# Zero matmuls between the last V product and the first scores, and token pairs on one partition: a fused attention and MLP block on one core

## The chip, the cores and the metric

The kernel runs on one core of a Trainium2 chip. The metric is device time in microseconds (us) of a whole execution. A profiled execution has a span, from its first instruction to its last, and a time of its own that lies a little above it.

The engines are named as the profile names them: PE is TensorE's matmuls and PEld its weight loads, DVE is VectorE, ACT is ScalarE, POOL is GpSimd, and SPq is SyncE's queue, which issues every DMA here.

## The reference

Input x has 2048 tokens of 512 features, in bf16. It is normalised, and attention with one shared K and V head and a GELU MLP are both applied to the same normalised x; both results are added to x.

```python
xn = _layernorm(x)                                    # 2048 x 512
# A: 32 query heads of 16, one K head and one V head
q = (xn @ wq).reshape(B, S, 32, 16)
k, v = xn @ wk, xn @ wv                               # 2048 x 16 each
p = softmax(einsum("bhqd,bkd->bhqk", q, k) * 16 ** -0.5)
a = einsum("bhqk,bkd->bhqd", p, v).reshape(B, S, 512) @ wo
# B: 512 -> 1792 -> 512
m = gelu(xn @ w1 + b1) @ w2 + b2
out = x + a + m
```

## The kernel before

**Stages.** A prologue loads x (16 tiles of 128 tokens), normalises it, transposes it (xnT), and makes K, V and the first group's Q. The main loop follows: 4 blocks of 512 queries, 8 groups of 4 heads in each, 16 key tiles. A tile of work is 128 keys by 512 queries of one head, and three tiles make a unit `u`, of which there are 683. For each unit TensorE computes scores into three banks of PSUM (`scores`, line 1009: three matmuls on different rows of the array), the exponential of two thirds of them is done on ScalarE (`exp`, line 1032) and of the rest on VectorE and GpSimd by integer arithmetic (`Dt`, lines 1063, 1106, 1110), and TensorE multiplies with V into one accumulator bank (`pv_mm`, line 1076). Banks 0 to 2 take the even units' scores and banks 3 to 5 the odd ones'. The Q, MLP and output products of each block (line 682) are spread among the units at due times; two GELU passes on ScalarE stand at units 182 and 512.

**What sets the order.** A recorder, `Prog`, collects every instruction with what it reads and writes. `Prog.schedule` then plays the program against a table of durations and due times and fixes one order for each engine. `Prog.emit` writes that order out, with one semaphore for each engine and for each DMA stream, so that at run time each engine works through its own list and waits where the list says so. The scheduler knows one kind of work that no data needs: `filler` and `pro_filler`, matmuls with a tile of zeros. In the prologue it inserts `pro_filler` (512 columns into bank 3) until the last V product has been placed (`s_seen`), in the main loop `filler`. Between the last V product and the first scores it inserts nothing.

**The prologue in its order.** SyncE issues nine loads of x, two with one tile and seven with two tiles, then wk, wv, wq, w1 (rows of 1792 elements), b1, w2, wo. A tile's statistics are taken on VectorE (line 782, then `mv`, line 796) or ScalarE (line 779); the reciprocal root is made on ScalarE (`lnv` and `rstd`, lines 800 and 802); the normalised tile is written by VectorE (line 815) or ScalarE (line 814), transposed by TensorE (line 827) and copied to `xnT` (line 831). V products are `v_tiles` (line 896, recorded at line 676). At the end the largest |k|, needed for the exponent's bias, is found: VectorE reduces to `kmx` (line 944), TensorE transposes it (line 945), VectorE reduces to `kmr` (line 947), TensorE spreads it over the partitions with `crow` (line 948, recorded at line 676), VectorE makes the bias `krow` (line 949), and only then is K copied to `KT` with the bias added (lines 849 and 850), on which the first scores wait. ScalarE writes V to its table meanwhile (line 962), and GpSimd writes five scaled copies of it (line 967).

**Tokens and partitions.** Token `t * 128 + p` lies on partition `p` of tile `t`, so a load of two tiles reads two runs of 1 KB for each partition:

```python
x_view = xf.rearrange("(t p) d -> p t d", p=P)
o, src, w = x_sb[:, a:b, :], x_view[:, a:b, :], [("x", ti) for ti in range(a, b)]
```

In the main loop x is loaded again, tile by tile (`x_load`), to be added to the output, and each output tile is stored as it is done (`store`).

Of the kernel before, what the change touches and what calls it, by code (L numbers as in the profile page):

```python
# [10 lines left out]
P = 128  # L11
# [42 lines left out]
LAL = 30.0  # L54
LCO = 0.0
PRO_FROM = 2.0
TBL = 1
DMASK = {".": (), "0": (0,), "2": (2,), "a": (0, 1), "b": (1, 2), "x": (0, 1, 2),
         "o": (0,), "t": (2,), "A": (0, 1), "B": (1, 2), "X": (0, 1, 2)}
# [55 lines left out]
class Prog:  # L115
# [116 lines left out]
    def schedule(self):  # L232
# [16 lines left out]
        order = []  # L249
# [22 lines left out]
        def seen(o):  # L272
            return max(o.rdy + (PL_TAKE if o.kind == "pl" else 0.0), lockend) if o.lock else o.rdy

        while left:
            best_e, best_t = None, None
            for e in engs:
# [5 lines left out]
                t = max(free[e], min([seen(o) for o in able[e]] if not pro else [0.0]))  # L283
# [3 lines left out]
            e, t = best_e, best_t  # L287
            cand = [o for o in able[e] if seen(o) <= t + 1e-9]
            if e == "pe":
                op = self.pick_pe(t, cand, ready["pe"], mode, visit, cgbusy)  # L290
                st = max([free["pe"]] + cgbusy) if mode == "col" else max([free["pe"], pend + SWITCH] + cgbusy)
# [3 lines left out]
                lim = min([o.rdy for o in ready["pe"] if o.kind == "S"] + [t + 9.0]) if op is None else t  # L295
                if op is None and self.pro_filler and not s_seen and st < PRO_FROM:
                    free["pe"] = st + 0.05
                    continue
                if op is None and self.pro_filler and not s_seen and low:
                    f = _Op()  # L300
                    f.eng, f.stream, f.amt, f.need, f.ticket, f.kind = "pe", "pe", 1, False, None, "fill"
                    f.deps, f.fn, f.tag = list(self.fill_deps), self.pro_filler, (None, 0)
                    pace = [o for o in order[-40:] if o.eng in ("dve", "act") and o.vis <= st]
                    if pace:
                        pace = max(pace, key=lambda o: o.vis)
# [22 lines left out]
                if FILL_GAP and tgt and low and st > FILL_FROM and lim - st > FILL_GAP:  # L328
                    for cg in range(4):
                        f = _Op()  # L330
# [15 lines left out]
                if op == "idle":  # L346
                    op = None
# [4 lines left out]
            else:  # L352
                op = min(cand, key=self.due)
# [40 lines left out]
            if e == "pe":  # L394
                vleft -= op.kind == "v"
                s_seen = s_seen or vleft == 0
                st = t
                if op.kind in ("pv", "side"):
                    cg = op.tag[1]
                    st = max(t, cgbusy[cg], free["pe"])  # L400
                    if mode != "col":
                        st = max([t, pend + SWITCH] + [c + SWITCH for c in cgbusy])
# [17 lines left out]
                elif op.kind != "side":  # L420
                    m = {"S": "row", "side": "col"}.get(op.kind, "full")
                    w = SWITCH if m != mode else 0.0
                    st = max([t, pend + w] + [c + w for c in cgbusy])
# [30 lines left out]
            for o, cross in op.outs:  # L454
                o.nun -= 1
                v = op.vis if cross else op.end
                if v > o.rdy:
                    o.rdy = v
                if o.nun == 0:
                    ready[o.eng].append(o)  # L460
        last = {}
        for op in order:
            if op.kind == "pv":
# [6 lines left out]
        self.ncold = ncold  # L470
        self.span = max(o.vis for o in order)
        self.ops = order

    def settle(self):
        free = {e: 0.0 for e, _ in self.SECTIONS}
        mode, cg, pend, aend = None, [0.0] * 4, 0.0, 0.0
        for op in self.ops:
            occ = op.occ
            lat = 0.0 if op.kind == "fill" else op.lat
            t = max([free[op.eng]] + [o.real for o in op.deps])  # L480
            if op.eng == "pe":
                if op.kind in ("pv", "side") or (op.kind == "fill" and occ > 0.15):
                    t = max(t, cg[op.tag[1]]) if mode == "col" else max([t, pend + SWITCH] + [c + SWITCH for c in cg])
                    cg[op.tag[1]] = t + 0.216
                    mode, end = "col", t + 0.006
                else:
                    m = "row" if op.kind == "S" else "full"
                    w = SWITCH if m != mode else 0.0
                    t = max([t, pend + w] + [c + w for c in cg])
                    mode, end = m, t + occ  # L490
                pend = t + occ
            else:
                end = t + occ
            free[op.eng] = max(free[op.eng], end)
            op.real = t + occ + lat
            if op.kind in ("exp", "gelu"):
                aend = max(end + A_LAG, aend + occ + A_INC)
                op.real = aend + A_SEM
# [47 lines left out]
def bass_parallel_sum__grouped_kv_mqa__dense_activation_gelu__prompt_kernel(  # L546
# [13 lines left out]
    xf = A_x.flatten_outer_dims()  # L560
    of = out.flatten_outer_dims()
    S, D = xf.shape
# [17 lines left out]
    with ExitStack() as es:  # L580
        def sb(shape, dtype, name):
            return es.enter_context(nc.sbuf_tensor(name, shape, dtype))

        x_sb = sb([P, NT, D], bf, "x_sb")
# [19 lines left out]
        zeros = sb([P, P], bf, "zeros")  # L604
# [46 lines left out]
        def bank(b, n=1):  # L651
            return pAll[:, b * 512:(b + n) * 512]

        pO, pM = bank(6), bank(7)
        pr = Prog(nc)
# [3 lines left out]
        def B(b):  # L659
            return ("bank", b)  # L660
# [27 lines left out]
        def dma(eng, o, i, stream, r=(), w=(), lat=2.2, allow=1.0, occ=0.7, **kw):  # L688
            return add(eng, lambda e: e.dma_start(o, i), r, w, dma=stream, occ=occ, lat=lat, allow=allow, **kw)
# [6 lines left out]
                return act(fa, r=ra, w=w, n=na, lat=la, due=due, tag=alt)  # L696
            return dve(fd, r=rd, w=w, n=nd, mode=mode, due=due, tag=alt)

        x_view = xf.rearrange("(t p) d -> p t d", p=P)
        nd = 0  # L700
        for a, b, t in X_D:
            nd += 1
            if a is None:
                o, src, w = ((wvk[:, :, Dh:2 * Dh], A_wk, ["wk_s"]), (wvk[:, :, 0:Dh], A_wv, ["wv_s"]))[b]
                src = src.rearrange("(k p) n -> p k n", p=P)
            else:
                o, src, w = x_sb[:, a:b, :], x_view[:, a:b, :], [("x", ti) for ti in range(a, b)]
            dma("sp", o, src, f"d_i{nd}", w=w, lat=t - 0.47 * nd, due=0.0, occ=0.47)
        dma("sp", wq_sb[:], A_wq.rearrange("(k p) n -> p k n", p=P), "d_wq", w=["wq"], due=0.4, lat=8.0)
        dma("sp", w1_sb[:], B_w1.rearrange("(k p) n -> p k n", p=P), "d_w1", w=["w1"], due=0.5, lat=9.0)  # L710
# [3 lines left out]
        def setup(fn, r=(), w=(), occ=0.16, due=0.0, lat=0.1, **kw):  # L714
# [20 lines left out]
              w=[(k, g, j) for k in ("QT", "QTm") for g in range(NGR) for j in range(HG)])  # L735
        setup(lambda e: e.tensor_copy(wkp[:, :, :, 0:Dh], wvk[:, :, Dh:2 * Dh].unsqueeze(2).to_broadcast([P, DT, 4, Dh])),
              r=["wk_s", "wkp"], w=["wkp"], occ=0.35, due=2.0)
# [8 lines left out]
              r=["mrow"], w=["isc"], due=10.0)  # L746
# [10 lines left out]
        for gl in range(2):  # L757
            setup(lambda e, gl=gl: e.tensor_copy(sel_diag[gl], mask8[:, 4 * gl:4 * gl + 4].unsqueeze(1).to_broadcast([P, NGR // 2, HG])),
                  r=["mask8", "sel8"], w=["sel8"], due=12.0)
# [96 lines left out]
        def vbank(a, b):  # L856
            return (pO[:, a * 32:b * 32], "O") if a < NVA else (bank(5)[:, (a - NVA) * 32:(b - NVA) * 32], B(5))
# [32 lines left out]
        def vsrc(a, b):  # L890
            return vbank(a, b)[0].rearrange("p (t n) -> p t n", n=32)[:, :, 0:Dh]
# [49 lines left out]
        for ft, bk in H_PRO:  # L941
# [8 lines left out]
            r=["khm", "kcm"], w=[B(3), "kb", "krow"], n=40, due=0.0)  # L950
# [5 lines left out]
        for va, vb_ in ((0, NVA), (NVA, NT)):  # L956
            src = vsrc(va, vb_)
            ad(lambda e, src=src, va=va, vb_=vb_: e.activation(Vf[:, va:vb_, :], src, ACT.Copy),
               lambda e, src=src, va=va, vb_=vb_: e.tensor_copy(Vf[:, va:vb_, :], src), (vb_ - va) * Dh, (vb_ - va) * Dh,
               w=[vbank(va, vb_)[1], ("Vf", va)], due=DU["vf"])  # L960
            r = ["V1", ("Vf", va)]
            ad(lambda e, va=va, vb_=vb_: e.activation(V1[:, 0, va:vb_, 0:Dh], Vf[:, va:vb_, :], ACT.Copy),
               lambda e, va=va, vb_=vb_: e.tensor_copy(V1[:, 0, va:vb_, 0:Dh], Vf[:, va:vb_, :]), (vb_ - va) * Dh, (vb_ - va) * Dh,
               w=[("V", 0, va)], ra=r, rd=r, mode=2, due=DU["vf"] + 0.1)
        for v in KV_ORD:
            c = SPL_C[v]
            f = lambda e, v=v, c=c: e.tensor_scalar(V1[:, 1 + v, :, 0:Dh], Vf, c, None, ALU.mult)
# [282 lines left out]

        def x_load(tb, i):
            ti = tb * 4 + i
            dma("sp", x_sb[:, 14 + i % 2, :], x_view[:, ti, :], f"d_xr{i % 2}", w=[("x", 14 + i % 2)], lat=2.5)

        def store(tb, i, src, key):
            ti = tb * 4 + i
            dma("sp", of[ti * P:(ti + 1) * P, :], src, f"d_o{i}", r=[key], w=[("ob", i)])

        def out_tile(tb, i):
            y_mm(tb, i, al=Y_ALLOW)  # L1260
            wo_mm(tb, i, range(NGR // 2), al=Y_ALLOW)
            b2_mm(al=Y_ALLOW)
            xr, key = x_sb[:, 14 + i % 2, :], ("x", 14 + i % 2)
            dve(lambda e: e.tensor_tensor(xr, pM, xr, ALU.add), w=[key] + M4, allow=EV_ALLOW)
            store(tb, i, xr, key)
# [100 lines left out]
        for i in range(4):  # L1366
            mm4(bank(FB[i]), oT[:, i * P:(i + 1) * P], wol[:, :], False, True,
               r=[("oTl", i // 2), "wol"], w=[B(FB[i])], due=0.0)
        for i in (0, 1, 3, 2):
            dst, key = ub[:, 6 + i, :], ("u", 0, 6 + i)  # L1370
            w = [(B(FB[i]), j) for j in range(4)] + ([B(FB[i])] if i < 3 else []) + [key]
            if i < 3:
                dve(lambda e, i=i, dst=dst: e.tensor_tensor(dst, bank(FB[i]), xpy[:, i, :], ALU.add),
                    r=[("u", 0, 2 * i), ("u", 0, 2 * i + 1)], w=w)
            else:
                act(lambda e, i=i, dst=dst: e.activation(dst, bank(FB[i]), ACT.Copy), w=w)
            store(tb, i, dst, key)
        pr.in_chain = False
        if PRO_FROM:
            zr = bass.AP(zeros[:].tensor, zeros[:].offset, [list(zeros[:].ap[0]), [0, 4], [1, P]])  # L1380
            pr.pro_filler = lambda e: e.matmul(bank(3), zeros[:], zr, start=True, stop=True, skip_group_check=True)
        if FILL_GAP:
            pr.filler = lambda e, j, o: e.matmul((pO if o else pM)[32 * j:32 * j + 32, :], zeros[:, 0:32], xnT[:, 0, 0:TBW],  # L1383
                                                 start=not o, stop=not o, skip_group_check=True,
# [37 lines left out]
```

## Time and profile before

| | us |
|---|---|
| median of 3 runs | 748.96 |
| lowest and highest | 748.05, 751.28 |
| profiled execution, its own time | 749.08 |
| its span | 747.4 |
| PE, DVE, ACT, POOL busy | 732.1, 731.5, 730.2, 384.6 |
| mean granted TensorE clock | 0.993 of full speed |

In the profile a row of the timeline gives the start, the length, the engine, the line, what is written and read, how many instructions are merged, and in brackets how long the engine was idle before it and what released it. Line 676 stands for all ordinary matmuls of the prologue and line 682 for the products in column groups, since helpers record them; the operands tell them apart. Line 1381 is `pro_filler`. A row of windows gives for a stretch of time how long each engine was busy in it; PEclk is the share of TensorE's full clock that was granted. A busy time of matmuls includes the tail of each one.

### The profile page before, as it was taken

The numbers are of one execution on the slowest core, as the hardware profiler recorded it, in microseconds if no ns is written. First come the engines' busy times: TensorE is split into PE (matmuls) and PEld (weight loads), VectorE is DVE, ScalarE is ACT, GpSimd is POOL, SyncE is SP. The second block draws the span as 40 slices with busy tenths as digits, with TensorE's granted clock in tenths as the row PEclk, the third lists the DMA queues.
The fourth block names the chain that finished last, engine by engine and source line by source line (L and its number), as shares of the span: only waits on it lengthen the run. The fifth ranks groups of instructions, "written<-read, shape, count | busy, mean of one in ns | idle before, by whom it ended". The sixth has DMA issues, their size and how long they took to land.

```text
span 747.4 us, 22083 instructions
## 1 busy us (share of the span) xinstructions
PE 732.1 (98%) x9033; PEld 214.1 (29%) x9033; DVE 731.5 (98%) x1412; ACT 730.2 (98%) x741; POOL 384.6 (51%) x548
## 2 busy tenths in 40 slices
PE   8999999999999999999999999999998999999998
PEld 4222222222233222222222222222232222222223
DVE  7899999999999999999999999999999999999996
ACT  7799999999999999999999999999999999999995
POOL 7434555555533556555656455444544656546560
PEclk9899999999999999999999999999999999999999
DMA  9200100000020010100101010100100101010011
GB/s 302 71 15 22 28 13 17 24 9 17 16 46 22 18 38 18 23 17 14 25 14 27 25 39 16 36 18 14 24 13 24 30 18 38 16 46 18 10 31 36
DMA packets 32094, 23.34 MB, mean 31 GB/s; under 512 B 16385, under 2 KB 27514, under 8 KB 31994
## 3 DMA queue, kind: packets, MB, share of 16 engines
q1 hardware_dynamic: 31994, 21.94, 11.3%
q8 instruction: 72, 1.18, 0.7%
q14 instruction: 28, 0.23, 0.1%
HBM read 13.08 MB, written 2.35 MB: 21 GB/s over the span
## 4 chain that ended last, share of the span: by engine, by line
ACT 61%; PE 23%; DVE 15%; issue 1%; DMA 0%; SPq 0%
ACT E L1032 61%; PE pAll L1076 10%; PE pAll L1009 7%; DVE Dt L1063 6%; PE pAll L682 5%; DVE Dt L1110 5%; DVE stats L782 1%; PE pAll L676 1%; DVE ub L815 1%; DVE Of L1122 1%; DMA x_sb<-in_A_x_dram 0%; PE pAll L1383 0%; DVE Dt L1106 0%; DVE x_sb L1218 0%; DVE xnT L831 0%
## 5 line engine op out<-in xcount | busy, mean ns | idle before, releaser
L1032 ACT ACTIVATE E<-pAll 128x1024 bf16<-128x1024 f32 (+1 forms) x676 | 681.0, 1277 | 3.5 <-PE pAll L1009 3.4
L1106 POOL TENSOR_SCALAR Dt<-Dt 128x512 int16<-128x512 int16 x454 | 343.6, 757 | 327.0 <-DVE Dt L1110 117.6
L1076 PE MATMUL pAll<-Dt,V 128*32 128x512 bf16 x2775 | 409.7, 385 | 2.6 <-DVE Of L1122 2.3
L1063 DVE TENSOR_SCALAR Dt<-pAll 128x512 int16<-128x512 f32 (+1 forms) x541 | 368.9, 696 | 3.7 <-PE pAll L1009 2.6
L1076 PE MATMUL pAll<-E,V 128*32 128x512 bf16 x1493 | 304.5, 384 | 0.2 <-DVE Of L1122 0.2
L1110 DVE TENSOR_SCALAR Dt<-Dt 128x1024 int16<-128x1024 int16 (+6 forms) x540 | 289.4, 562 | 0.4
L1009 PE MATMUL pAll<-QT,KT 32*128 32x512 bf16 x2048 | 268.0, 386 | 5.2 <-ACT E L1032 2.1
L1009 PEld LDWEIGHTS pAll<-QT,KT 32*128 32x128 bf16 x2048 | 66.6, 91 | 296.5 <-ACT E L1032 282.6
L1076 PEld LDWEIGHTS pAll<-Dt,V 128*32 128x32 bf16 x2775 | 103.2, 95 | 102.7 <-issue 69.1
L1076 PEld LDWEIGHTS pAll<-E,V 128*32 128x32 bf16 x1493 | 72.7, 94 | 44.6 <-issue 33.5
L682 PE MATMUL pAll<-xnT,w_sb 128*32 128x512 bf16 x896 | 84.8, 383 | 0.0
L682 PE MATMUL pAll<-w_sb,x_sb 128*32 128x512 bf16 x448 | 76.4, 384 | 0.0
L682 PE MATMUL pAll<-w_sb,ub 128*32 128x512 bf16 x448 | 64.3, 383 | 0.1
L682 PE MATMUL pAll<-wop,oTp 128*32 128x512 bf16 x256 | 51.9, 383 | 0.0
L1153 POOL TENSOR_TENSOR oTp<-OfP,rbP 128x256 bf16<-128x256 f32 (+1 forms) x28 | 22.5, 809 | 14.6 <-DVE Dt L1110 7.9
L682 PEld LDWEIGHTS pAll<-xnT,w_sb 128*32 128x32 bf16 x896 | 21.3, 95 | 26.8 <-issue 17.0
L682 PE MATMUL pAll<-xnT,wq_sb 128*32 128x512 bf16 x256 | 26.8, 383 | 0.0
L1106 DVE TENSOR_SCALAR Dt<-Dt 128x512 int16<-128x512 int16 x101 | 26.5, 284 | 0.0
L1122 DVE COPY Of<-pAll 128x512 f32<-128x512 f32 x31 | 21.2, 682 | 0.1
L1218 DVE TENSOR_SCALAR x_sb<-pAll,b1T 128x512 bf16<-128x512 f32 x28 | 20.8, 742 | 0.0
L1218 DVE TENSOR_SCALAR ub<-pAll,b1T 128x512 bf16<-128x512 f32 x28 | 20.7, 739 | 0.0
L682 PEld LDWEIGHTS pAll<-w_sb,x_sb 128*32 128x32 bf16 x448 | 18.3, 94 | 8.2 <-issue 6.7
(123 smaller groups left out, 264.5 us busy)
## 6 DMA issues: line engine op xcount, KB each, us to landing
OfP<-Of SPq DMA_DIRECT2D x124, 32.0 KB, 2.0
rbP<-rden_rows SPq DMA_DIRECT2D x124, 32.0 KB, 1.8
w_sb<-in_B_w_dram SPq DMA_DIRECT2D x2, 1792.0 KB, 11.3
x_sb<-in_A_x_dram SPq DMA_DIRECT2D x18, 128.0 KB, 2.2
QT<-qp SPq DMA_DIRECT2D x124, 16.0 KB, 1.8
x_sb<-in_A_x_dram SPq DMA_DIRECT2D x7, 256.0 KB, 4.4
out_dram<-x_sb SPq DMA_DIRECT2D x12, 128.0 KB, 2.0
wq_sb<-in_A_wq_dram SPq DMA_DIRECT2D x1, 512.0 KB, 5.8
```

Of the source, the lines that this page charges most:

```text
L676: return add("pe", lambda e: e.matmul(o, l, rh, start=start, stop=stop, **kw), r, w, occ=occ, lat=dlat[1], allow=allow, **ak)
L682: add("pe", lambda e, c=c, j=j: e.matmul(o[c, :], l[:, c], rh, start=start, stop=stop, tile_position=(0, 32 * j)), r, [(k, j) for k in w] ...
L782: dve(lambda e, ti=ti, c=c: e.bn_stats(stats[:, c, :], x_sb[:, ti, :]), r=[("x", ti)], w=[("st", ti)], n=557, due=land(ti) + DU["sd"])
L1009: ins = e.matmul(o, l, rh, start=True, stop=True, tile_position=(q0, 0))
L1032: o = act(lambda e: e.activation(E[:, s0:s0 + na, :], bank(b0, na).rearrange("p (a n) -> p a n", a=na), ACT.Exp, scale=LN2 / 128.0), w=[B( ...
L1063: op = dve(lambda e: e.tensor_scalar(Dt[:, s:s + n, :], bank(bk, n).rearrange("p (a n) -> p a n", a=n), float(127 * 128) + SPL_D, SPL_MIN, ...
L1076: add("pe", lambda e, a, b: e.matmul(pO[32 * j:32 * j + 32, :], V1[:, v, kt, :], rhs, start=a, stop=b, tile_position=(0, 32 * j)), r=r + [ ...
L1106: add("pool", lambda e, d=d, k=k: e.tensor_scalar(d, d, 1.0, float(k), ALU.mult, ALU.add), [], [(("D", base[o > 0] + q), o)], occ=PL_OCC, ...
L1110: dve(lambda e, d=view(o, nb), q=view(i, nb), k=k: e.tensor_scalar(d, q, float(k), None, ALU.add), r=keys(i), w=keys(o), n=nb * n * TBW, m ...
L1122: dve(lambda e: e.tensor_copy(Of[:, i, :], pO), w=["O", ("Of", i)], allow=0.0)
L1153: "pool", lambda e, c=c: e.tensor_tensor(oTp[0:n, sl, c], OfP[0:n, s, c], rbP[0:n, s, c], ALU.mult),
L1218: dve(lambda e: e.tensor_scalar(ubs[tb % 2][:, ft, :], pM, b1T[:, ft:ft + 1], None, ALU.add), r=["b1T"], w=M4 + [ukey(tb, ft)], n=TBW + 57 ...
```

## The change

**Fill.** After the order is fixed, a new pass, `fill_gaps`, walks through it. From the last V product to the first scores it puts as many zero matmuls of 256 columns into each planned gap of TensorE as fit at 0.13 us each. They write to half of bank 2, which the first scores overwrite. Each waits for the newest VectorE or ScalarE instruction that should be done by then, so that it runs at its place in the gap and not ahead of it.

**Tokens.** Tokens 2p and 2p+1 of a block of 256 now lie on partition p, in two neighbouring tiles. A load of two tiles reads one run of 2 KB for each partition. A single tile, and a store, moves rows of 1 KB that lie 2 KB apart. Attention does not depend on the order of the keys, and queries go back to their own tokens in the store.

```diff
+GAP_BANK = 2
...
+        order = self.fill_gaps(order)
...
+    def fill_gaps(self, order):
+        t0 = min(o.start for o in order if o.kind == "S")
+        t1 = max(o.end for o in order if o.kind == "v")
+        ew = [o for o in order if o.eng in ("dve", "act") and o.start < t0]
+        s0 = min((o for o in order if o.kind == "S"), key=lambda o: o.start)
+        out, end = [], None
+        for op in order:
+            if op.eng == "pe" and op.start <= t0:
+                if end is not None:
+                    for i in range(int((op.start - end - 0.1) / 0.13)):
+                        st = end + 0.05 + 0.13 * i
+                        f = _Op()
...
+                        f.deps, f.fn, f.tag = list(self.fill_deps), self.gap_filler, (None, 0)
+                        f.occ = 0.107
+                        f.start, f.end, f.vis = st, st + f.occ, st + f.occ + 0.2
+                        pace = [o for o in ew if o.vis <= st]
+                        if pace:
+                            pace = max(pace, key=lambda o: o.vis)
+                            pace.need = True
+                            f.deps.append(pace)
+                        f.deps += [o for o in s0.deps if o.vis <= st and o.eng != "pe"]
...
+                        out.append(f)
+                if op.start >= t1:
+                    end = max(end or 0.0, op.start + op.occ)
+            out.append(op)
+        return out
...
-        x_view = xf.rearrange("(t p) d -> p t d", p=P)
+        x_view = xf.rearrange("(t p a) d -> p t a d", p=P, a=2)
+        o_view = of.rearrange("(t p a) d -> p t a d", p=P, a=2)
...
-                o, src, w = x_sb[:, a:b, :], x_view[:, a:b, :], [("x", ti) for ti in range(a, b)]
+                o, src, w = x_sb[:, a:b, :], (x_view[:, a // 2, :, :] if b - a == 2 else x_view[:, a // 2, a % 2:a % 2 + 1, :]), [("x", ti) for ti in range(a, b)]
...
-            dma("sp", x_sb[:, 14 + i % 2, :], x_view[:, ti, :], f"d_xr{i % 2}", w=[("x", 14 + i % 2)], lat=2.5)
+            dma("sp", x_sb[:, 14 + i % 2, :], x_view[:, ti // 2, ti % 2, :], f"d_xr{i % 2}", w=[("x", 14 + i % 2)], lat=2.5)
...
-            dma("sp", of[ti * P:(ti + 1) * P, :], src, f"d_o{i}", r=[key], w=[("ob", i)])
+            dma("sp", o_view[:, ti // 2, ti % 2, :], src, f"d_o{i}", r=[key], w=[("ob", i)])
...
+            zg = bass.AP(zeros[:].tensor, zeros[:].offset, [list(zeros[:].ap[0]), [0, 2], [1, P]])
+            pr.gap_filler = lambda e: e.matmul(bank(GAP_BANK)[:, 256:512], zeros[:], zg, start=True, stop=True, skip_group_check=True)
```

TensorE's list before, from the last eight V products to the second set of scores (`tk_dve`, `tk_act` and `tk_pool` are the semaphores of VectorE, ScalarE and GpSimd; `kmx` and `kmr,crow` are the two small matmuls of the maximum; the four between are a K product):

```order
L676 MATMUL pAll<-wvk,xnT 128x32 x7
L676 MATMUL pAll<-xnT,oTp 128x512 x4
L945 MATMUL pAll<-ident_f,kmx 1x128 [waits tk_dve]
L676 MATMUL pAll<-kmr,crow 128x1 [waits tk_dve]
L1009 MATMUL pAll<-QT,KT 128x512 [waits tk_dve]
L1009 MATMUL pAll<-QT,KT 128x512 x2
```

The same place in the changed kernel:

```order
L708 MATMUL pAll<-wvk,xnT 128x32 x7
L708 MATMUL pAll<-xnT,oTp 128x512 x4
L978 MATMUL pAll<-ident_f,kmx 1x128 [waits tk_dve]
L1415 MATMUL pAll<-zeros 128x256 [waits tk_act]
L1415 MATMUL pAll<-zeros 128x256
L1415 MATMUL pAll<-zeros 128x256 [waits tk_act]
L708 MATMUL pAll<-kmr,crow 128x1 [waits tk_dve]
L1415 MATMUL pAll<-zeros 128x256 x4
L1415 MATMUL pAll<-zeros 128x256 [waits tk_dve]
L1415 MATMUL pAll<-zeros 128x256
L1042 MATMUL pAll<-QT,KT 128x512 [waits tk_dve]
L1042 MATMUL pAll<-QT,KT 128x512 x2
```

Three fills stand ahead of the `kmr,crow` matmul and six behind it. The first waits for ScalarE's first write of V to its table (line 962 before), the third for its second write, the eighth for `krow`. Every other row of TensorE's list keeps its place, and the lists of VectorE, ScalarE and GpSimd are the same in both kernels.

On SyncE's list the loads of x change their shape, here before:

```order
L689 DMA x_sb<-in_A_x_dram 128x512 x2
L689 DMA x_sb<-in_A_x_dram 128x2x512 x7
L689 DMA wvk<-in_A_wk_dram 128x4x16
L689 DMA wvk<-in_A_wv_dram 128x4x16
L689 DMA wq_sb<-in_A_wq_dram 128x4x512
```

and in the changed kernel:

```order
L721 DMA x_sb<-in_A_x_dram 128x512 x2
L721 DMA x_sb<-in_A_x_dram 128x1024 x7
L721 DMA wvk<-in_A_wk_dram 128x4x16
L721 DMA wvk<-in_A_wv_dram 128x4x16
L721 DMA wq_sb<-in_A_wq_dram 128x4x512
```

Seven loads go from 256 runs of 512 elements to 128 runs of 1024, and nothing on SyncE's list moves.

More of the change, by code (lines that the diff above doesn't have):

```diff
@@ L472, in schedule @@
         self.ops = order
+    def fill_gaps(self, order):
[10 more added lines that the diff above has]
+                        f = _Op()
+                        f.eng, f.stream, f.amt, f.need, f.ticket, f.kind = "pe", "pe", 1, False, None, "fill"
+                        f.deps, f.fn, f.tag = list(self.fill_deps), self.gap_filler, (None, 0)
[7 more added lines that the diff above has]
+                        f.deps += [o for o in s0.deps if o.vis <= st and o.eng != "pe"]
+                        for o in f.deps:
+                            o.need = True
+                        out.append(f)
[3 more added lines that the diff above has]
+        return out
     def settle(self):
```

## The prediction

> **What bounds the kernel now.** I read the page first, then the chain that ended last in order of time, then busy time by windows of 3.4 us, then the timeline of the places that these pointed at.
>
> ```profile
> PE 732.1 (98%) x9033; PEld 214.1 (29%) x9033; DVE 731.5 (98%) x1412; ACT 730.2 (98%) x741; POOL 384.6 (51%) x548
> ACT 61%; PE 23%; DVE 15%; issue 1%; DMA 0%; SPq 0%
> ```
>
> From the page: three engines are busy 98% of the span, and the chain changes between them. The main loop has no slack to win, and the change touches nothing in it. What the change can move is the stretch ahead of it: the loop starts earlier, or its first microseconds run faster. The chain of waits in order of time shows what that stretch hangs on (start, length, what):
>
> ```profile
> 1.71 3.53 DMA x_sb<-in_A_x_dram
> ...
> 5.26 1.29 DVE stats L782 x2
> ...
> 20.04 0.61 DVE xnT L831
> ...
> 23.11 0.36 DVE KT L850
> ...
> 29.07 0.54 PE pAll L1009 x3
> ...
> 30.42 0.35 PE pAll L1009 x3
> ...
> 30.79 1.45 ACT E L1032
> ```
>
> Three pieces: the third x load (tiles 2 and 3), issued at 1.71, which lands at 5.24; VectorE from 5.26 to 20.65 without a break (every piece left out there is DVE); then TensorE, from the first scores, once KT is made at 23.11, up to the sixth exp at 30.79. In that last piece a score step costs 0.54 on the chain, and at 30.42 only 0.35. The windows say why (length; busy us of PE, PEld, DVE, ACT, POOL with counts; granted TensorE clock; DMA share; GB/s):
>
> ```profile
> core 0: us, PE busy (x) PEld busy (x) DVE busy (x) ACT busy (x) POOL busy (x), PEclk, DMA share, GB/s
> 9.60:13.00 3.40, 2.71 (x46) 1.94 (x43) 3.40 (x10) 3.21 (x9) 3.09 (x16) 1.00 1.07 377
> 19.80:23.20 3.40, 2.04 (x22) 0.94 (x22) 2.44 (x9) 1.58 (x9) 1.13 (x2) 1.00 0.77 244
> 23.30:26.60 3.30, 3.08 (x14) 0.70 (x14) 2.17 (x5) 2.50 (x4) 3.14 (x6) 0.50 0.03 10
> 26.60:30.00 3.40, 3.40 (x16) 0.55 (x14) 2.31 (x4) 2.32 (x3) 0.94 (x2) 0.50 0.05 10
> 30.10:33.50 3.40, 3.40 (x36) 0.98 (x34) 3.40 (x7) 3.29 (x4) 0.53 (x1) 1.00 0.04 10
> 565.90:569.30 3.40, 1.14 (x23) 0.60 (x25) 3.40 (x7) 3.38 (x3) 0.00 (x0) 1.00 0.04 10
> 569.40:572.70 3.30, 3.30 (x30) 1.47 (x22) 3.30 (x7) 3.07 (x3) 0.00 (x0) 0.50 0.09 21
> ```
>
> The clock was halved from 23.2 to 30.0, after a stretch of 3.4 us in which TensorE was busy for 2.04 only. Stretches with 2.71 and more kept it whole. It was halved once more at 569.4, after a stretch with 1.14. So the threshold lies between 2.04 and 2.71 by this measure.
>
> **The fill.** It adds nine matmuls of 256 columns and takes nothing away. TensorE's timeline in the gap:
>
> ```profile
> 20.91 1.02 PE L676 MATMUL pAll<-xnT,oTp 128*128 128x512 bf16 x4
> 21.94 0.27 PE L945 MATMUL pAll<-ident_f,kmx 128*1 128x128 f32 x1
> 22.58 0.17 PE L676 MATMUL pAll<-kmr,crow 1*128 1x1 bf16 x1 [0.38 <-DVE kmr L947]
> 23.52 1.03 PE L1009 MATMUL pAll<-QT,KT 32*128 32x512 bf16 x6 [0.76 <-DVE KT L850]
> ```
>
> Four matmuls of 512 columns take 1.02, and of that about 0.17 is the tail (the one of a single column takes 0.17), so 0.21 for 512 columns, and 0.107 for 256. Three fills stand in the 0.38 of idle time (0.32), six in the 0.76 (0.64). Before 23.20 the gap leaves 0.38 and 0.45 idle; with both filled, 2.04 becomes some 2.8, on the side of 2.71. Fills are zeros, and zeros count, as the program's start shows:
>
> ```profile
> 8.34 1.02 PE L1381 MATMUL pAll<-zeros 128*128 128x512 bf16 x3 [0.47 <-ACT lnv L800]
> ```
>
> At 8.34 three matmuls of 512 columns take 1.02, and two waits lie among them. At half clock they would be 3 x 0.43 and a tail, 1.46. Behind them lie only the zero matmuls and four transposes, so zeros had brought the clock up.
>
> What the halved clock costs is read from ScalarE, with GpSimd's copies of V beside it:
>
> ```profile
> 21.58 0.67 ACT L962 ACTIVATE V<-oTp 128x224 bf16<-128x224 f32 x2
> 24.17 1.94 ACT L1032 ACTIVATE E<-pAll 128x1024 bf16<-128x1024 f32 x2 [0.38 <-PE pAll L1009]
> 26.53 1.02 ACT L1032 ACTIVATE E<-pAll 128x1024 bf16<-128x1024 f32 x1 [0.42 <-PE pAll L1009]
> ...
> 29.66 2.58 ACT L1032 ACTIVATE E<-pAll 128x1024 bf16<-128x1024 f32 x2 [0.48 <-PE pAll L1009]
> ```
>
> ```profile
> 24.91 2.71 POOL L967 TENSOR_SCALAR V<-oTp 128x256 bf16<-128x256 f32 x3
> ```
>
> At full clock the first scores are done 0.2 earlier (0.54 against 0.35), so the first exp starts at 23.97. Two exps back to back take 1.94, one alone 1.02: 0.92 each. The sixth then starts at 23.97 + 5 x 0.92 = 28.57 instead of 30.79: 2.2 us. TensorE is not late: its 7.27 us from 23.52 to 30.79 shrink to 3.6, against 4.6 of exps. VectorE was idle for 3.30 - 2.17 and 3.40 - 2.31 in the two stretches at half clock, 2.2 together, so it too can come 2.2 earlier and no more. GpSimd's copies of V end 24.91 + 0.9 for the first of three, at 25.8; the V products that wait for it stand just ahead of the score step of 29.07 and come some 1.5 earlier, to about 26.5, so they are covered by 0.7. I take 2.1. The bounds are 0 (the clock falls anyway) and 2.2.
>
> What the fills may cost: the third waits for ScalarE's second V write, which ends at 22.25, and the crow matmul behind it (22.58) starts the chain krow, KT, first scores. With the fill itself, 0.107, that is 22.36, and 0.2 of cover is left, less what the semaphore takes. The eighth waits for krow; at 23.11 KT is made from krow, in 0.36, and the first scores wait for that, so the last two fills (0.21) fit in ahead of them. So nothing at full clock, and up to 0.5 at half clock, where six fills take 1.28 and not 0.64.
>
> A rule against it: the Trainium skill, "TensorE: Matmul & The Clock Gate", section "Why this matters for your kernels", asks for no idle gaps over about 3 us between bursts. By it the clock had no cause to fall here, and the fill would bring nothing. The trace does not agree: the longest idle in this gap is 0.76, and the clock fell.
>
> **The x loads.** Seven loads keep their 256 KB but carry 128 runs of 2 KB instead of 256 of 1 KB; two carry 128 runs of 1 KB as before, now 2 KB apart. Their times to landing, the rate while x comes and while w1 (3.5 KB runs) comes, and one wait of ScalarE between 5.2 and 23.6:
>
> ```profile
> x_sb<-in_A_x_dram SPq DMA_DIRECT2D x7, 256.0 KB, 4.4
> x_sb<-in_A_x_dram SPq DMA_DIRECT2D x2, 128.0 KB, 2.2
> ```
>
> ```profile
> 5.00:6.00 1.00, 1.00 (x3) 0.15 (x1) 0.73 (x2) 0.83 (x3) 0.97 (x9) 1.00 1.04 357
> 12.00:13.00 1.00, 1.00 (x29) 0.93 (x25) 1.00 (x3) 0.81 (x4) 0.85 (x6) 1.00 1.01 401
> ```
>
> ```profile
> ACT lnv L800 <- DVE mv L796: 0.5, 1, 0.5
> ```
>
> From the rate alone: 256 KB at 357 GB/s take 0.73, at 401 0.65; the third load gains some 0.1. From the shape: with 128 runs a load lands 2.2 after its issue, and 128 KB more at 357 add 0.4, so the third could land at 1.71 + 2.6 = 4.3, 0.9 earlier than 5.24. VectorE follows by as much, but ScalarE only by the 0.5 that it waits for VectorE's mv near 8.0; beyond that ScalarE is late next. I take 0.5, bounds 0 and 0.9. The reloads of x and the stores (128 KB, 1 KB rows in both versions) keep their sizes; the loads are issued six steps ahead, so I cost them at nothing, and no row shows a stride of this kind; a tenth of their 2.2 to landing either way, 0.2, bounds it, and it can show in the last store alone.
>
> Another rule against it: the Trainium skill, "DMA: Bandwidth & Descriptors", Specifications, puts line rate at 512 B and more. By it runs of 1 KB lose nothing, the x part is 0, and the sum would be 747.0. The trace agrees only in part: 357 against 401 GB/s.
>
> **Sum.** The profiled execution took 749.08 (span 747.4 and 1.7 around it), 0.12 above the median shown. 749.08 - 2.1 - 0.5 = **746.5**, or 0.33% under the median. It reaches the end whole, since from 30 on every engine's order is unchanged and all three are full.
>
> **Rivals.**
>
> (a) The fill does not hold the clock, or the fall comes at another stretch. For it: the clock is whole again at 30.0, 6.8 us after the fall, two stretches of 3.4; that the stretches run from a fixed point of the program no row shows, so their edge need not lie at 23.20 in every execution. Against: any such stretch over the gap gains most of the 0.96 of fills. Time 749.08 - 0.5 = 748.6. The rule on idle gaps gives the same.
>
> (b) The second fall, at 569.4, goes too, because the stall before it now lies differently to the stretches. It costs 3.4 us at half speed on a chain that TensorE carries, 1.7. Time 746.5 - 1.7 = 744.8. For it: the program comes 2.6 earlier; against: TensorE is idle there for over 2 us, and most positions catch that.
>
> (c) Slower: the clock is low already when the fills come. Then they stand in front of the crow matmul and the first scores at 0.21 each: 0.1 to 0.2 and 0.5, and the loads give nothing: 749.8. It decides from an edge before about 22.4. Should the clock then stay low for two more stretches, each costs between 1.05 (the 2.1 above, over two) and 1.7 (half of 3.4): 751.9 to 753.2. For it: nothing in this trace, whose clock fell after the gap; against: VectorE and ScalarE run the transposes' chain at full length until 20.6, and the stretch at 9.60, of the same work, held the clock.
>
> (d) The loads land no earlier, and the fill works: 749.08 - 2.1 = 747.0. For it: the rate of 357 is near 401 already; against: 2.2 against 3.53 to landing at equal queues ahead. This is the result that the rule on line rate gives.
>
> **Chances.** Forecast 0.44, (a) 0.14, (b) 0.22, (c) 0.10, (d) 0.10. A measurement of this kernel tells about 0.5% from no change, 3.7 us: 745.2 and 752.7. Faster by more: most of (b) and the edge of the forecast, as the times shown spread over 3.2 us: 0.25. Slower by more: the upper half of (c), 0.05. Within: 0.70. The range runs from 744.6 (just under (b)) to 749.2 (over (a), and no change), leaving out (c) and the tails; (d) lies inside.
>
> **What would show it.** Right: granted clock 1.00 from 6.2 through 33; the wait of exp for scores gone after the first; sixth exp near 28.1; third x load landing at 4.3 to 5.1, first scores near 23.0. Wrong: 0.50 anywhere in 23 to 30; first scores at 23.5 or later; fills between 22.2 and 23.5 that end after KT is ready; a gain at 30 us that is gone at the end.

## The result, and the profile after

| | before | after |
|---|---|---|
| median of 9 runs each, one chip, us | 748.43 | 746.71 |
| lowest and highest | 747.16, 751.28 | 745.02, 747.12 |
| profiled execution, its own time | 749.08 | 746.57 |
| its span | 747.4 | 744.8 |
| mean granted TensorE clock | 0.993 | 0.998 |
| start of the first, 11th and last exp | 24.17, 35.83, 737.06 | 23.88, 33.35, 734.52 |

The ratio is 0.9972, with a 95% interval from 0.9959 to 0.9986: 0.28% less, and less than the 0.5% that the prediction took as telling. The forecast of 746.5 and its range hold. The exps already say where the gain lies: 0.29 us before the first one, 2.19 between the first and the 11th, 0.06 in all the rest. Of the 0.29, 0.08 lies ahead of the first scores (23.52 before, 23.44 after) and 0.21 behind them, where the first exp now waits 0.16 for scores instead of 0.38 and no later one waits:

```profile
23.88 7.86 ACT L1065 ACTIVATE E<-pAll 128x1024 bf16<-128x1024 f32 x8 [0.16 <-PE pAll L1042]
```

The sixth exp starts at 28.41; the prediction had put it near 28.1. The busy time by windows of the kernel after has the same columns as before:

```profile
9.60:13.00 3.40, 2.43 (x44) 1.78 (x41) 3.40 (x11) 3.21 (x8) 2.83 (x14) 1.00 1.06 393
19.80:23.20 3.40, 2.58 (x25) 1.32 (x23) 2.35 (x9) 1.58 (x8) 1.21 (x2) 1.00 0.64 204
23.30:26.60 3.30, 3.26 (x25) 0.91 (x23) 3.14 (x6) 3.14 (x4) 3.14 (x6) 1.00 0.03 6
26.60:30.00 3.40, 3.40 (x34) 0.95 (x29) 3.40 (x7) 3.40 (x5) 0.85 (x2) 1.00 0.05 15
562.10:565.50 3.40, 1.35 (x21) 0.43 (x18) 3.40 (x7) 3.40 (x2) 0.34 (x1) 1.00 0.04 11
565.60:568.90 3.30, 3.11 (x31) 1.31 (x34) 3.30 (x7) 3.27 (x3) 0.00 (x0) 0.50 0.10 24
```

From 19.80 to 23.20 TensorE's 2.04 of busy time became 2.58, the clock stayed whole through 30, and ScalarE, busy for 2.50 and 2.32 in the two halved stretches before, is now full. The second fall is still there, now from 565.5. TensorE's timeline in the gap, with the fills at L1415:

```profile
21.86 0.27 PE L978 MATMUL pAll<-ident_f,kmx 128*1 128x128 f32 x1
21.97 0.53 PE L1415 MATMUL pAll<-zeros 128*128 128x256 bf16 x3
22.50 0.17 PE L708 MATMUL pAll<-kmr,crow 1*128 1x1 bf16 x1
22.61 0.84 PE L1415 MATMUL pAll<-zeros 128*128 128x256 bf16 x6
23.44 0.72 PE L1042 MATMUL pAll<-QT,KT 32*128 32x512 bf16 x6
```

The fills stood in nobody's way: from the kmx matmul to crow it is 0.64 in both kernels (21.94 to 22.58 before), from crow to the first scores 0.94 in both. But those scores start at 23.44 instead of 23.52, though the third x load was forecast to bring 0.5. By the trace it did land 0.6 earlier, at 4.64, and VectorE began with it at 4.66 instead of 5.26:

```profile
4.66 1.29 DVE L815 BATCH_NORM_STATS2 stats<-x_sb 128x6 f32<-128x512 bf16 x2 [0.71 <-DMA x_sb<-in_A_x_dram]
```

The chain in order of time shows where that went:

```profile
7.96 8.80 DMA b1row<-in_B_b_dram
...
16.81 0.18 PE pAll L708
...
17.30 0.69 DVE xnT L864
```

And TensorE's timeline at that place, after and then before:

```profile
16.81 0.18 PE L708 MATMUL pAll<-ident,b1row 14*128 14x14 bf16 x1 [0.49 <-DMA b1row<-in_B_b_dram]
```

```profile
16.89 0.18 PE L676 MATMUL pAll<-ident,b1row 14*128 14x14 bf16 x1
```

The small product with b1 stands among the transposes, and its load stands behind w1 in the queue. TensorE waited 0.49 us for it, and the transposes behind it waited too. Before, the same product ran at 16.89 without a wait. The loads themselves got faster in these two profiles, by the groups of DMAs (median to landing, 4.4 before):

```profile
x_sb<-in_A_x_dram SPq DMA_DIRECT2D x7, 256.0 KB, 3.9
```

One number of every execution helps from here on: its mean granted clock. A fall is from here on one stretch of 3.41 us at half clock, so that the 6.8 us behind the gap before the change are two. One fall is 0.23% of the span, and the two profiles fit: three falls at 0.993, one at 0.998. So 1.000 is an execution without a fall, 0.998 or 0.997 one, and 0.995 and less two and more. In the later series the kernel before ran 86 times: 7 times with none (median 746.5), 33 with one (747.76), 26 with two (748.6), 10 with three (749.83), 10 with four (751.2); the median of all is 748.29. The profiled execution, with three, was one of its slower ones.

### The profile page after: what moved, and what is told of

Read it like the earlier page. It is cut to its first block, busy times and chain, and to the rows that moved or that the text cites. A ratio compares the mean times of both kernels' runs of the same rounds, so it can differ in the third digit from the quotient of the medians.

```text
span 744.8 us, 22099 instructions
## 1 busy us (share of the span) xinstructions
PE 730.0 (98%) x9040; PEld 215.0 (29%) x9042; DVE 731.1 (98%) x1412; ACT 729.7 (98%) x741; POOL 383.1 (51%) x548
## 3 DMA queue, kind: packets, MB, share of 16 engines
q1 hardware_dynamic: 31098, 21.94, 11.2%
## 4 chain that ended last, share of the span: by engine, by line
ACT 62%; PE 22%; DVE 13%; DMA 1%; SPq 1%; issue 1%
ACT E L1065 62%; PE pAll L1109 10%; PE pAll L1042 6%; DVE Dt L1096 6%; PE pAll L714 5%; DVE Dt L1143 5%; DMA b1row<-in_B_b_dram 1%; SPq L721 1%; DVE Of L1155 1%; PE pAll L708 0%; PE pAll L1418 0%; DVE Dt L1139 0%; DVE x_sb L1251 0%; DVE xnT L864 0%; DVE qp L1223 0%
```

## Experiments

The edits are to the changed kernel. A table of all runs follows the single accounts.

**Fill alone (e1_fill_only).** x goes back to runs of 1 KB; so do the reload and the store.

```diff
-        x_view = xf.rearrange("(t p a) d -> p t a d", p=P, a=2)
...
+        x_view = xf.rearrange("(t p) d -> p t d", p=P)
...
```

> The fill without the token pairs: x is loaded in 1 KB runs as before. Theory: the whole gain is the clock that stays up after the gap, and the loads give 0.1 at most, so the time is that of the changed kernel, 746.7 (1.7 under the kernel before), with the first exp near 23.95 and the sixth near 28.5. Rival: the loads carry a part that shows only later; then this one stays 0.5 behind the changed kernel, at 747.2.

Measured: 747.85, ratio 1.0002 [0.9992, 1.0012]. None of its 11 executions has two falls, but at one fall it is no faster than the kernel before (747.89 against 747.76). In its profile the third x load lands at 4.51, earlier than before, but from the fifth on the loads are late (7.56, and 6.68 before), and so is b1 behind them:

```profile
18.37 0.18 PE L708 MATMUL pAll<-ident,b1row 14*128 14x14 bf16 x1 [0.96 <-DMA b1row<-in_B_b_dram]
```

By the counts, 0 of 11 against 16 of 35 executions with two falls and more, the fill removes falls; its worth in the median is no more than the falls that are there to remove, and 748.08 to 747.85 is not told from nothing by the interval. This was the first sign that the forecast's split was off.

**Pairs alone (e2_pairs_only).**

```diff
-        order = self.fill_gaps(order)
```

> The token pairs without the fill. Theory: the third load lands near 4.6 and VectorE starts 0.6 earlier, but the b1 product on TensorE waits for its load until about 16.8, so the first scores come at 23.45 and the clock is halved after them: 748.3, no more than 0.1 under the kernel before. Rival: earlier loads are worth 0.5 at the end: 747.9.

Measured: 746.85, ratio 0.9988 [0.9973, 1.0003]. Five of 11 executions have two falls or more, up to 750.35; the profiled one had none, though nothing filled its gap. At one fall its median is 746.6, 1.2 under the kernel before. So without the fill the fall after the gap comes in some executions and not in others. The profile shows how: one window of 3.4 us over its gap is emptier than the one of 2.04 before, and the clock stayed whole.

```profile
20.60:24.00 3.40, 1.86 (x24) 0.76 (x20) 2.44 (x9) 1.84 (x8) 1.47 (x2) 1.00 0.48 154
```

In every profile that records them, the clock changes come at whole steps of 3.413 us from the first one. Counted so, an edge lay at 23.23 before (first change at 6.16), and nearly all of the gap was inside one stretch; here (first change at 4.88) an edge lies at 21.95 and cuts the gap in two, with 2.79 and 2.27 of busy time in the stretches on its sides.

**b1 earlier (e3_b1_early).** One due time of the prologue puts the b1 load ahead of w1 and its product four rows earlier in TensorE's list.

```diff
-PRO_DUE = (0,0,0,0,0,0,0,0,0,0,0,0.4,0.5,0.6,0.7,1017.1, ...
+PRO_DUE = (0,0,0,0,0,0,0,0,0,0,0,0.4,0.5,0.45,0.7,1017.1, ...
```

> The changed kernel with the small b1 load issued ahead of w1 on SyncE's list, and the b1 product four rows earlier on TensorE's. Theory: the b1 load was the next wait, so the 0.6 of the earlier x loads now reaches the first scores: 22.95 instead of 23.44, and the time is 746.2. Rival: something else is late in between (w1 lands later, ScalarE's statistics, the fills' own waits), and the first scores stay within 0.15 of 23.44: 746.6.

Measured: 746.36, ratio 0.9975 [0.9962, 0.9988]; the wait for b1 is gone and the first scores start at 23.10. Against the changed kernel that is 0.35, which the overlapping intervals do not tell from nothing.

**Short fills (e4_short_fill).** The same nine matmuls, with 32 columns instead of 256.

```diff
-            zg = bass.AP(zeros[:].tensor, zeros[:].offset, [list(zeros[:].ap[0]), [0, 2], [1, P]])
...
+            zg = bass.AP(zeros[:].tensor, zeros[:].offset, [list(zeros[:].ap[0]), [0, 2], [1, 16]])
...
```

> The changed kernel with fills of 32 columns instead of 256: the same nine matmuls with the same waits, at an eighth of the streaming. Theory: the clock goes by how long TensorE is busy in a stretch of 3.4 us, nine times 0.013 is not enough, and the clock is halved after the gap in most executions: 748.3. Rival: it goes by how long TensorE is idle at a time, or the fills help by their waits alone; then this one is as fast as the changed kernel, 746.7.

Measured: 746.77, and 4 of 12 executions with two or three falls (747.07 to 749.29). Its timeline in the gap, from a profiled execution without a fall there:

```profile
21.71 0.44 PE L1415 MATMUL pAll<-zeros 128*128 128x32 bf16 x3
22.25 0.17 PE L708 MATMUL pAll<-kmr,crow 1*128 1x1 bf16 x1
22.36 0.27 PE L1415 MATMUL pAll<-zeros 128*128 128x32 bf16 x4
22.80 0.21 PE L1415 MATMUL pAll<-zeros 128*128 128x32 bf16 x2 [0.18 <-DVE krow L982]
23.18 0.72 PE L1042 MATMUL pAll<-QT,KT 32*128 32x512 bf16 x6 [0.17 <-DVE KT L883]
```

No idle time is left over 0.2 behind the last V product, and by their mean clock a third of the executions still had a second fall (only the one profile shows places, so that this fall followed the gap is inferred). That is not told from leaving the gap empty (46 of 86), and it is told from 256 columns (0 of 43). So what helps is the columns that stream, and not the short pauses alone. The Trainium skill, "TensorE: Matmul & The Clock Gate", section "Why this matters for your kernels", asks for no idle gaps over about 3 us between bursts of matmuls; that is not enough here, where the clock fell before the change behind pauses of 0.76 and less.

**Half fills (e8_half_fill).** 128 columns.

```diff
-            zg = bass.AP(zeros[:].tensor, zeros[:].offset, [list(zeros[:].ap[0]), [0, 2], [1, P]])
...
+            zg = bass.AP(zeros[:].tensor, zeros[:].offset, [list(zeros[:].ap[0]), [0, 2], [1, P // 2]])
...
```

> The changed kernel with its nine fills cut from 256 to 128 columns. If what counts is the columns streamed in a stretch of 3.4 us, the fills add half (9 x 0.053 = 0.48 us instead of 0.96): a stretch over the gap has 2.04 + 0.48 = 2.5 busy at most, between the 2.04 that fell and the 2.71 that held. Mean clock 0.997 to 0.998 in nearly all executions if 2.5 holds it, median 746.7; two or three falls (0.995, 0.993) in a third to a half of the executions, as with the fills of 32 columns, if it doesn't.

Measured: 746.58, one execution of 12 with two falls. Half the columns nearly suffice, and by 12 executions they are not told from all of them; the place of the threshold is not settled closer than that.

**b1 earlier with runs of 1 KB (e5_b1_early_runs1k).** The edits of the first and the third experiment together.

> The fill stays, x is read in runs of 1 KB as before the change, and the b1 load stands ahead of w1 with its small product four rows earlier. If the pairs gained their 1.2 us because the b1 load, behind x and w1 in the queue, came later with runs of 1 KB and held TensorE (18.37 us in the run with the fill only, 16.81 after the change), this kernel loses nothing: no wait of TensorE for b1row, first exp at 23.5 to 24.0, time within 0.3 of the 746.4 of the kernel with pairs and b1 early. Rival: the x loads themselves end later with runs of 1 KB and hold VectorE's and ScalarE's chain, whatever b1 does: first exp at 24.2 or later, time 747.2 to 747.9 like the fill alone.

Measured: 746.41, which looks like the theory, but 6 of its 12 executions had no fall against 3 of 11 with pairs. At one fall it is 747.16 (pairs with b1 early: 746.46), at none 746.06 (745.25). Its chain speaks for the rival:

```profile
2.70 5.04 DMA x_sb<-in_A_x_dram
7.74 0.02 issue
7.76 0.69 DVE stats L814
```

TensorE no longer waited for b1, and VectorE's chain began with the fifth x load, which landed at 7.74; first scores at 24.20. My theory that b1 was the whole way fell here. To divide it properly the falls had to go.

**A second fill (e6_second_fill).** 16 of the same matmuls go into the gap near 563, behind VectorE's last reading of bank 2.

```diff
+STALL_G, STALL_N = 24, 16
...
+        order = self.fill_stall(order)
...
+        i = next(n for n, o in enumerate(order) if o.kind == "pv" and o.tag[0] == STALL_G)
+        p = [o for o in order[:i] if o.kind == "p1"][-1]
...
+        return order[:i] + out + order[i:]
```

> The changed kernel with 16 more zero matmuls of 256 columns in TensorE's gap of 2.3 us near 563.4, ahead of the first V product of the next group. Theory: a fall of the clock costs 1.1 to 1.5 us wherever it comes, so with both gaps filled no execution has a fall: mean clock 1.000 in every one, median 745.0 to 745.6, that is 1.2 under the changed kernel. Rival one: the second fall lies beside other work and costs nothing: mean clock 1.000, time 746.4 to 746.9. Rival two: the fills keep TensorE from the V products behind them (16 x 0.107 = 1.7 in a gap of 2.3): the V product that starts at 565.79 now starts later, time 746.7 or above.

Measured: 745.41, ratio 0.9960 [0.9946, 0.9974], mean clock 1.000 in all 8 executions. Its timeline there, then its windows:

```profile
563.01 1.92 PE L1432 MATMUL pAll<-zeros 128*128 128x256 bf16 x16
565.42 0.39 PE L1126 MATMUL pAll<-Dt,V 128*32 128x512 bf16 x1 [0.49 <-DVE Of L1172]
```

```profile
562.10:565.50 3.40, 2.91 (x38) 1.83 (x34) 3.40 (x7) 3.40 (x2) 0.00 (x0) 1.00 0.06 14
565.60:568.90 3.30, 3.21 (x45) 1.51 (x39) 3.30 (x7) 3.27 (x4) 0.00 (x0) 1.00 0.11 27
```

The V product behind them still waits for the copy of the accumulator, 541.92 after the first exp at 23.50; after the change it was 541.91 (565.79 and 23.88). So the fills cost nothing, and with 2.91 of busy time instead of 1.35 the clock held. (This trace has no clock record, so its 1.00 is not a reading; the next kernel, with the same fills, has a record, whole from 7.08 to 744.36.) From the 11th exp to the last it is 700.24, against 701.17: this fall is worth 0.93. The five profiles with a fall here need 701.17 to 701.35 for that part, the eight without one 700.21 to 700.25, so 0.9 to 1.1; by the medians of the two kernels it is 1.3.

Three of those eight have no fill in this gap (pairs alone, half fills, b1 early with 1 KB). An edge of the stretches fell further inside the gap there: their emptiest stretch had 1.72, 1.65 and 1.77 of busy time and kept the clock, where 1.07 to 1.36 in the other five lost it.

**Second fill and b1 earlier (e7_second_fill_b1).**

The edits of the third experiment and of the last one.

> The same 16 fills in the kernel with the b1 load early. If the wait for b1 is worth what its profile showed (0.3 to 0.5 us) and the fall 1.2, this is the fastest: 744.7 to 745.2, mean clock 1.000 in every execution. If the wait for b1 was covered by VectorE's chain, it equals the kernel with the second fill alone within 0.2.

Measured: 745.38, ratio 0.9957 [0.9942, 0.9972], mean clock 1.000 in all 9. With runs of 2 KB the b1 load is worth nothing in the median: the 0.49 of the profile after was one execution's.

**The pairs without falls (e9_second_fill_runs1k, e10_second_fill_b1_runs1k, e11_second_fill_again).** Both fills and runs of 1 KB (the edit of the first experiment); the same with b1 early (that of the third); both fills with pairs; all on one chip.

> Both gaps filled, so that no fall of the clock blurs the comparison, and x in runs of 1 KB as before the change. The profiles so far put the first scores at 23.52, 24.99 and 24.20 with runs of 1 KB and at 23.06 to 23.98 with runs of 2 KB, 0.85 apart in the mean, so this kernel should take 0.8 to 1.1 more than the same with pairs (run again beside it): 746.2 to 746.5 against 745.4, and mean clock 1.000. Rival: the pairs are worth only the 0.08 that the first two profiles showed, and the 1.0 came from the falls: 745.4 to 745.6.

> The same with the b1 load ahead of w1. If the pairs gain by way of the b1 load, this is level with the kernel with pairs (745.4). If they gain by x itself, it stays with the kernel of 1 KB runs (746.2 to 746.5). With b1 early the run with one fill lay 0.7 under the fill alone at equal falls and 0.7 over the same with pairs, so I expect the middle: 0.3 to 0.6 under runs of 1 KB without it.

> The kernel with both gaps filled and pairs, once more, on the chip of the other two: 745.2 to 745.6, mean clock 1.000 in every execution.

Measured: 746.94, 746.20 and 745.53. The pairs are worth 1.4 by the medians (1.3 over executions without a fall), a little over what I expected; with runs of 1 KB b1 early brings 0.7 (0.6) of that, and the other 0.7 is x itself. Two of the first kernel's 12 executions had falls all the same (748.96 with two, 749.66 with one); where, no profile shows. The chain of the first and of the second kernel, in their own profiled executions:

```profile
8.83 8.29 DMA b1row<-in_B_b_dram
17.12 0.05 issue
17.16 0.18 PE pAll L725
...
24.23 1.94 ACT E L1081 x2
```

```profile
2.69 5.08 DMA x_sb<-in_A_x_dram
...
7.79 0.69 DVE stats L831
...
24.66 1.94 ACT E L1081 x2
```

and of the third, with pairs:

```profile
1.71 3.40 DMA x_sb<-in_A_x_dram
...
5.13 1.29 DVE stats L832 x2
...
23.81 2.85 ACT E L1082 x3
```

These are the two ways in which a later load reaches the exps: by b1 behind w1, or by a later x load at the head of VectorE's chain. Which of them decides changes from execution to execution. With both gaps filled the times without a fall spread over 1.5 and 2.0 us with runs of 1 KB, and over 0.4, 1.0 and 1.5 with pairs (the last with b1 early).

All runs by the number of falls; the three groups are one chip each, with the kernel before run beside them:

| kernel | median | two falls and more | median at one | at none |
|---|---|---|---|---|
| before | 748.08 | 16 of 35 | 747.76 | 746.65 |
| fill alone | 747.85 | 0 of 11 | 747.89 | 747.12 |
| pairs alone | 746.85 | 5 of 11 | 746.6 | 745.7 |
| b1 early | 746.36 | 0 of 11 | 746.46 | 745.25 |
| short fills | 746.77 | 4 of 12 | 746.77 | 745.29 |
| before | 748.28 | 14 of 28 | 747.4 | 746.1 |
| b1 early, 1 KB | 746.41 | 0 of 12 | 747.16 | 746.06 |
| second fill | 745.41 | 0 of 8 | none | 745.41 |
| second fill, b1 early | 745.38 | 0 of 9 | none | 745.38 |
| half fills | 746.58 | 1 of 12 | 746.9 | 745.93 |
| before | 749.13 | 16 of 23 | 747.7 | 746.65 |
| second fill, 1 KB | 746.94 | 1 of 12 | 749.66 | 746.81 |
| second fill, b1 early, 1 KB | 746.20 | 0 of 12 | none | 746.20 |
| second fill, pairs again | 745.53 | 0 of 6 | none | 745.53 |

The changed kernel itself: 0 of 9 with two falls, 746.72 at one, 745.02 at none.

## Why the prediction was right, and where not

**The fill holds the clock: right.** Of the 43 executions with the full fill in the first gap alone none has two falls, against 46 of 86 before. For the profiled execution the price was near: from the first scores to the sixth exp, which is what the sum's 2.1 stands for, it is 7.27 before and 4.97 after, 2.3 less. The first ten exps take 11.66 only in the profile before; in the other 12, none of which has a halved stretch there, they take 9.47 to 9.49. The price of the fills themselves, "nothing at full clock", is right by the timeline.

**But the term of 2.1 was mis-sized for the median.** The prediction took two falls at the gap and one later as given, since the profiled execution had them and lay 0.12 from the median of three runs. Of 86 executions 20 have three falls or more, and 40 have none or one. The stretches' edges lie at another offset each time (the first change to the whole clock came between 4.55 and 7.41 us in the 12 profiles that record it), and only some catch the gap. Nor is there one threshold of busy time, as the prediction read it between 2.04 and 2.71: 2.04 lost the clock at the first gap, and 1.65 to 1.77 kept it at the second. The sentence of rival (a) that the edge need not lie at 23.20 in every execution held for the kernel before, and was not turned on the forecast's own term. What the fill is worth in the median is not settled: the run with the fill alone gave 0.2, and its interval runs from 0.6 less to 0.9 more; the kernel before loses 748.29 - 747.76 = 0.5 to falls beyond the first; and the pairs, at 1.0 to 1.4, leave 0.3 to 0.7 of the 1.7. By each of these it is far under 2.1. Its main effect is on the slow end.

**The x loads: 0.5 was too little, by a way that was not the one named.** The prediction reckoned with the third load, from its shape. Over the profiles that load landed at 4.99 in the mean of five kernels with 1 KB and at 4.83 in eight with 2 KB, so most of the 0.6 of the first two profiles was those two executions. In the two profiles 0.08 came through to the first scores, since b1 behind w1 was late next; the prediction asked what is late next on ScalarE alone, and did not look at the queue behind x. Load by load the gain adds up: over the same profiles the ninth x load landed at 10.68 and at 9.88, w1 at 17.7 and 16.4, and the first scores started at 24.14 and 23.39. The first profile of before, at 23.52, was the earliest of its five, and that of after, 23.44, one of the later ones of its eight. By the executions without falls the pairs give 1.3. The upper bound of 0.9 was too low. The Trainium skill, "DMA: Bandwidth & Descriptors", Specifications, has line rate from 512 B on; by it, and by rival (d), the pairs would give nothing, and the runs do not agree.

The errors nearly cancel. The forecast took 2.1 + 0.5 = 2.6 off the profiled execution's 749.08; the median of nine runs before was 748.43, so 0.65 of the 2.6 lay in the starting point, and 1.7 was measured, of which the pairs are 1.0 to 1.4 and the fill the rest. That the time came out at 746.71, 0.2 from the forecast, is luck as much as working.

**Rival (b)** came in one of the 9 executions, at 745.02 with no fall; 8 kept one, in the profile at 565.5. Over the 43 executions with the first gap filled 12 have no fall, so its reason, another position of the gap to the stretches, was sound. Its price of 1.7 was too high: 0.9 to 1.1 by the exps and 1.3 by the medians. **Rival (c)** was not seen in any of the 43.

## What to carry to other kernels

A clock fall in one profile is a draw from a lottery: before it is priced, read how many executions have it from their mean clocks, and price it by that share. When a load gets faster, follow the whole queue behind it to the next small transfer that somebody waits for. Fill with matmuls that stream many columns, placed so that they are done before what the gap waits for arrives, and look for every gap that loses the clock: both gaps filled and pairs gave the best time here, 745.4 (0.9960 of before), within noise of the same with b1 early.

## What the runs showed of the hardware

- By the mean clocks two falls and more came in 4 of 12 executions with fills of 32 columns, which left no pause over 0.2 us in the gap, in one of 12 with 128 columns, and in none of 43 with 256 columns.
- The clock changes lie whole steps of 3.413 us apart, and the first comes at 4.55 to 7.41 us from the program's start. The same gap keeps the clock in one execution and loses it in another.
- A fall of one stretch at the second gap cost 0.9 to 1.1 us in the exps, though half of 3.41 is 1.7; two at the start of the loop cost 2.2 (11.66 against 9.47).
- With 128 runs of 2 KB instead of 256 of 1 KB the median of a two-tile load to landing was 3.9 instead of 4.4 us in the first two profiles, and the ninth x load landed 0.8 earlier in the mean of all. One load varies more than that between executions: the fifth landed between 6.11 and 7.56 with runs of 2 KB, between 6.68 and 7.77 with 1 KB.
